# A blocked causal attention with a feed-forward layer behind it: a stored order of issue in place of a list scheduler

## The chip, the cores and the metric

The kernel runs on one core of a Trainium2 chip. The metric is the device time of one execution in microseconds, taken as the median of the runs; lower is better. The engines are TensorE (PE; its weight loads PEld), VectorE (DVE), ScalarE (ACT), GpSimd (POOL) and SyncE (SP). Loads and stores are issued from the queues of SyncE and ScalarE.

## What is computed

Attention over 8 batches of 8 heads, 576 tokens of 64 dimensions, masked by blocks of 64 tokens, and on its output, as 4608 tokens of 512 dimensions, a layer of width 2048 with a hard gate:

```python
def _attn_ref(q, k, v):            # (8, 8, 576, 64) each
    ...
    scores = scale * np.matmul(q, k.transpose(0, 1, 3, 2))
    mask = block_i >= block_j      # blocks of 64
    scores = np.where(mask, scores, -1000000000.0)
    ...
    attn = attn / (np.sum(attn, axis=-1, keepdims=True) + 1e-09)
    return np.matmul(attn, v)

def _moe_ref(x, w_in, w_out):      # 4608x512, 512x2048, 2048x512
    h = x @ w_in
    relu6 = np.clip(h + 3.0, 0.0, 6.0)
    g = h * relu6 / 6.0
    return g @ w_out
```

## The kernel before

Matmuls run in f16 on operands that are split into a high and a low part: a product is three matmuls (high with high, high with low, low with high), and each f16 matmul step is a row of pairs, one matmul for each half of the array's 128 columns. The attention of batch 0 and the first feed-forward piece (192 tokens) run in f32.

The work is cut so. Attention goes by pairs of heads (`n`, 32 of them) and by three groups of query blocks (`g`): `s_group` (L1465) makes the scores `s`, their row maxima (`st`, VectorE), the exponentials (`p`, ScalarE), scaled probabilities split into halves (`phl`), which a DMA transposes (`pT`); `pv_group` (L1579) multiplies with V (`vhl`) into `x`. `qk_load` and `qk_prep` (L1205, L1216) load and split q and k (`qks`, `qkT`). For the first batch the steps with 32 in their names do the same in f32 (`qf`, `qr`, `qt`, `sf`, `pf`, `pt`, `pr`, `rd`). The feed-forward layer goes by 13 pieces of up to 384 tokens and 16 slices of the width: `ffn1` (L1793) makes `h`, the gate (`r`) and its halves (`g`); `ffn2` (L1841) adds up the output `o` over the 16 slices. Pieces 11 and 12 form `h` from seven half-sized products `m` for each pair of slices (`h_pair`, L1733; `w_comb`, `x_comb` prepare the sums `wr`, `wq`, `ws`, `xr`, `xt`). The weights come in 64-bit form (`rawi`, `rawo`, and pieces of `x` as a buffer), are converted (`exi`, `exo` on ScalarE; `sgi`, `sgo` on GpSimd or VectorE), scaled by reductions over the whole core (`gm`, `gs`, `mb`, `mt`) and split into `win` and `wout`.

None of this is issued as it is written. `Recorder` (L422) takes the place of the engines and records every call as a step (`Op`), with the steps that it depends on (`touch`, L556) and the engines that could run it (`ways`): scalings may run on VectorE, ScalarE and often GpSimd, loads may be issued from SyncE or ScalarE. Consecutive matmuls of one `joint` are one step. There are 6396 steps.

`schedule` (L644) then orders them by a list scheduler. It has a cost for each call (`cost`, L588) and keeps a clock for each engine; whichever engine's clock is lowest picks, among the steps whose inputs are there and whose tiles find a buffer, the one with the smallest due time. Due times come from the kernel's plan and from `SHIFT` (L78), a number for each group of steps; `LEAN` (L243) adds to the choice of engine where a step has several ways. On TensorE a change between steps that write half of the array's columns and steps that write all of them costs `TURN`, and the half ones are gathered in bursts. `emit` (L847) issues the steps in the order of their start, so every instruction stands under one line, L851. The framework keeps that order on each engine, gives each tile a buffer in that order, and adds the waits.

Of the kernel before, what the change touches and what calls it, by code (L numbers as in the profile page):

```python
# [17 lines left out]
P = 128  # L18
# [6 lines left out]
U = 2.211  # L25
# [30 lines left out]
LANES = 8  # L56
# [21 lines left out]
SHIFT = {  # L78
# [318 lines left out]


class Op:

    __slots__ = ("ways", "key", "grp", "lean", "preds", "joint", "n", "start", "end", "tiles", "eng", "half")


class Engine:


    def __init__(self, rec, name):
# [1706 lines left out]
```

## Time and profile before

| | us |
|---|---|
| median of 3 runs | 989.18 (988.69 to 990.63) |
| span of the profiled execution | 987.2 |
| TensorE busy | 965.6 |
| VectorE busy | 887.3 |
| ScalarE busy | 628.9 |
| GpSimd busy | 75.1 |

The span goes from the first to the last instruction of the profiled execution; the time of a run has some 2 us around it. A row of a group names the line, the engine, the operation, the tile written and those read, their shapes and the count; then busy time, mean ns of one, and the idle time of the engine just before with what ended it. Names have their buffer numbers left out.

### The profile page before, as it was taken

To read this page: it belongs to the slowest core of one execution; us is meant where nothing else is said; L and a number is where in the kernel's file an instruction comes from. 1 tells how busy PE (TensorE), PEld (TensorE's weight loads), DVE (VectorE), ACT (ScalarE), POOL (GpSimd) and SP (SyncE) were. 2 spreads that over 40 slices of the span, in tenths; PEclk is the share of its full clock that TensorE was granted. 3 is DMA by queue.
4 is the path that set the end of the run, shared out by engine and by line. 5 is a ranking of instruction groups with operands and counts; after the bars stand their busy time and mean duration, and the time that the engine had idled before them with its cause. 6 is when DMAs were issued, how large, how long until landed. Compare 5 with 4: busy or idle time off the path is not lost.

```text
span 987.2 us, 31085 instructions
## 1 busy us (share of the span) xinstructions
PE 965.6 (98%) x12585; PEld 722.1 (73%) x12585; DVE 887.3 (90%) x2450; ACT 628.9 (64%) x1527; POOL 75.1 (8%) x242
## 2 busy tenths in 40 slices
PE   6899999999999999999999999999999999999998
PEld 5666567767778866776677776777677787878885
DVE  6999999999999999999999899988979879977864
ACT  4788877676676666777784766665667554534422
POOL 1133200000000000000000000000100102000000
PEclk9999999999999999999999999999999999999999
DMA  8965567979789799898999686776667451000000
GB/s 233 308 210 157 103 124 137 188 127 214 113 155 199 125 181 160 135 188 149 160 168 170 110 174 124 125 150 123 128 131 135 79 101 36 2 34 2 34 3 33
DMA packets 407183, 129.02 MB, mean 131 GB/s; under 512 B 393984, under 2 KB 396544, under 8 KB 407040
## 3 DMA queue, kind: packets, MB, share of 16 engines
q1 hardware_dynamic: 397520, 118.84, 63.0%
q10 hardware_dynamic: 9520, 8.21, 2.8%
q8 instruction: 98, 1.61, 0.7%
q14 instruction: 45, 0.37, 0.1%
HBM read 45.09 MB, written 9.44 MB: 55 GB/s over the span
## 4 chain that ended last, share of the span: by engine, by line
PE 70%; DVE 5%; ACT 1%; issue 1%; DMA 0%; SPq 0%; DVEq 0%; ACTq 0%
PE o L851 30%; PE h L851 24%; PE m L851 6%; PE s L851 5%; PE pv L851 5%; DVE st L851 1%; DVE phl L851 1%; ACT p L851 1%; DVE r L851 1%; DVE qks L851 1%; DMA qk<-in_k_dram 0%; DVE g L851 0%; DVE vhl L851 0%; DVE qkmx L851 0%; DVE x L851 0%
## 5 line engine op out<-in xcount | busy, mean ns | idle before, releaser
L851 PE MATMUL o<-wout,g 128*64 128x512 f16 (+3 forms) x3336 | 404.5, 378 | 0.0
L851 PE MATMUL h<-x,win 128*64 128x384 f16 (+2 forms) x3952 | 356.2, 319 | 1.7 <-DVE r L851 1.2
L851 PEld LDWEIGHTS <-win 128*64 128x64 f16 (+1 forms) x4440 | 270.0, 110 | 60.0 <-issue 4.2
L851 PEld LDWEIGHTS <-g 128*64 128x64 f16 x3360 | 218.8, 110 | 107.7
L851 ACT ACTIVATE p<-s,st,esc 128x384 f32<-128x384 f32 (+4 forms) x280 | 163.0, 587 | 62.7 <-DVE st L851 47.0
L851 ACT ACTIVATE r<-h,eg,sh 128x384 f32<-128x384 f32 (+1 forms) x192 | 112.0, 600 | 71.5 <-PE h L851 67.6
L851 DVE SCALAR_TENSOR_TENSOR phl<-p,st,phl 128x384 f16<-128x384 f32 (+4 forms) x252 | 138.6, 589 | 0.5 <-ACT phl L851 0.4
L851 DVE TENSOR_REDUCE st<-s 128x1 f32<-128x384 f32 (+4 forms) x280 | 117.8, 447 | 10.2 <-PE s L851 8.8
L851 DVE SCALAR_TENSOR_TENSOR g<-r,g 128x384 f16<-128x384 f32 (+1 forms) x192 | 102.9, 541 | 5.1 <-ACT g L851 3.9
L851 ACT ACTIVATE g<-r 128x384 f16<-128x384 f32 (+1 forms) x135 | 67.7, 506 | 53.7 <-DVE r L851 27.5
L851 DVE SCALAR_TENSOR_TENSOR r<-r,eg,h 128x384 f32<-128x384 f32 (+1 forms) x160 | 93.7, 588 | 7.4 <-ACT r L851 7.1
L851 PE MATMUL s<-qkT 128*64 128x512 f16 (+7 forms) x1120 | 96.6, 287 | 2.2 <-ACT p L851 2.1
L851 ACT ACTIVATE phl<-p,st 128x128 f16<-128x128 f32 (+4 forms) x147 | 77.2, 563 | 28.3 <-DVE st L851 15.6
L851 PEld LDWEIGHTS <-vhl 128*64 128x64 f16 x1680 | 72.0, 110 | 9.5 <-issue 2.3
L851 PEld LDWEIGHTS <-qkT 128*64 128x64 f16 x1120 | 58.8, 110 | 24.9 <-issue 4.9
L851 PE MATMUL pv<-pT,vhl 128*64 128x192 f16 (+2 forms) x1680 | 73.0, 233 | 1.3 <-ACT x L851 0.8
L851 POOL MEMSET p<- 128x64 f32 x140 | 22.8, 163 | 529.5 <-DVE phl L851 460.0
L851 ACT ACTIVATION_READ_ACCUMULATOR p<-s,st,esc 128x1 f32 x280 | 55.2, 197 | 0.0
L851 ACT ACTIVATE r<-hf,eg,sh 128x192 f32<-128x192 f32 (+1 forms) x48 | 26.4, 592 | 40.7 <-DVE hf L851 39.3
L851 DVE SCALAR_TENSOR_TENSOR qks<-qk,rs_q,qks 128x576 f16<-128x576 f32 x56 | 45.8, 834 | 0.1
L851 DVE TENSOR_SCALAR phl<-p,st 128x512 f16<-128x512 f32 (+4 forms) x105 | 41.8, 419 | 1.1 <-DVE st L851 0.2
L851 PE MATMUL m<-x,ws 128*64 128x192 f16 x768 | 39.0, 246 | 0.0
(191 smaller groups left out, 1036.6 us busy)
## 6 DMA issues: line engine op xcount, KB each, us to landing
out_dram<-osb SPq DMA_DIRECT2D x34, 256.0 KB, 2.4
qk<-in_q_dram SPq DMA_DIRECT2D x28, 288.0 KB, 3.8
qk<-in_k_dram SPq DMA_DIRECT2D x26, 288.0 KB, 4.5
vnat<-in_v_dram SPq DMA_DIRECT2D x58, 128.0 KB, 3.2
rawo<-in_moe_w_out_dram SPq DMA_DIRECT2D x9, 512.0 KB, 5.8
x<-in_moe_w_in_dram SPq DMA_DIRECT2D x5, 512.0 KB, 6.2
pT<-phl SPq DMA_TRANSPOSE x140, 3.7
rawi<-in_moe_w_in_dram SPq DMA_DIRECT2D x4, 512.0 KB, 6.0
```

Source lines behind the costliest of these rows:

```text
L851: getattr(eng, method)(*args, **kw)
```

## The change

`SHIFT`, `LEAN`, the costs and the list scheduler go. In their place stands `ORDER`, a packed table with one entry of two bytes for each of the 6396 steps: thirteen bits are the step's number as recorded, three bits its engine. `schedule` unpacks it and hands out the steps in that order, each on the engine that the table names. The recorder, the steps, their tiles and the plan that records them are the same. What differs on the chip is the place of a step in its engine's queue, and for some the engine:

| steps on | before | table |
|---|---|---|
| TensorE | 2108 | 2108 |
| VectorE | 2444 | 2240 |
| ScalarE (with loads) | 1219 | 1328 |
| GpSimd | 236 | 312 |
| SyncE (loads, stores, transposes) | 389 | 408 |

ScalarE's queue begins in the table with loads of `qf` (k, q), then `vnat` three times and `qf` (q) twice; after these seven comes its first step of work. SyncE's begins with one load of `vnat`, then `qf` (q, k, k, k) and the first weight piece `rawi`. In the trace of before ScalarE's queue begins with two loads of `vnat`, SyncE's with one.

```diff
--- before.py
+++ after.py
@@ -75,332 +75,144 @@
-SHIFT = {
-    0: -94, 2: 115, 3: -347, 4: -33, 5: -62, 6: -65, 7: 144, 8: 268, 11: -175, 12: 150, 13: 13, 14: -134,
...
-LEAN = {
-    20: (-1145, 0), 50: (1084, 0), 60: (195, 0), 70: (-42, 0), 80: (0, -166), 82: (0, -194), 83: (-32, 0),
...
+ORDER = (
+    "c-l=^1wb2Jv&B7-1g%jVLWm2rK!M;EAqifJyK99~+}-Q$Za_=j-Q7!D>h9Fu+zovHo9y1bGjq<Fxf`;A-#9~~@l@JETRRF_XR?;5"
...
+    "a5Q5i(+idHusKF`kf}Hz^-v?(aWpTZ8jVU}L8H;IEQsVn$4ZR#0}7#-KUQF@q|yHnGO$r-Z)h*1d;brADM2a"
+)
 class Op:
 
-    __slots__ = ("ways", "key", "grp", "lean", "preds", "joint", "n", "start", "end", "tiles", "eng", "half")
+    __slots__ = ("ways", "preds", "joint", "n", "eng")
...
 class Recorder:
     NAMES = ("tensor", "vector", "scalar", "gpsimd", "sync")
-    LAT = {"tensor": 855, "vector": 37, "scalar": 39, "gpsimd": 65, "sync": 65}
-    TURN = 95
-    BIAS = {"vector": 250.0, "gpsimd": 500.0}
-    EDGE = 0.0
-    BURST, PATIENCE = 3, 4000.0
-    POLL = {"tensor": 1.0, "vector": 20.0, "scalar": 20.0, "gpsimd": 150.0, "sync": 100.0}
-
     def __init__(self, nc):
         self.nc = nc
         self.ops = []
-        self.key = 0.0
-        self.cls = ""
-        self.grp = 0
-        self.part = {}
+        self.key, self.cls, self.grp = 0.0, "", 0
         self.joint = None
-        self.adv = ADV
-        self.share = 2
         for n in self.NAMES:
             setattr(self, n, Engine(self, n))
         self.hist = {}
-        self.meta = {}
-        self.users = {}
 
     @staticmethod
     def box(a):
...
@@ -517,33 +305,12 @@
         last = self.ops[-1] if self.ops else None
         if eng == "tensor" and self.joint is not None and last and last.joint == self.joint:
             op = last
-            calls, occ, _, _ = op.ways[eng]
-            more, took, _ = self.cost(eng, method, args, kw, outs, ins)
-            op.ways[eng] = (calls + [(method, args, kw)], occ + more, occ + took, False)
+            op.ways[eng].append((method, args, kw))
         else:
             op = Op()
-            op.joint, op.n, op.ways = None, len(self.ops), {}
...
-            op.key = self.key - self.adv.get((eng, self.cls), 0.0) 
-            op.grp = self.grp + (10000 if eng == "tensor" else 20000 if ways[0][1] == "dma_start" else 0)
-            op.key += 0.1 * SHIFT.get(op.grp, 0)
-            op.lean = self.BIAS
-            if len(ways) > 1:
-                part = self.part[op.grp] = self.part.get(op.grp, -1) + 1
-                dv, dp = LEAN.get(10 * op.grp + part, (0, 0))
-                if dv or dp:
-                    op.lean = dict(vector=self.BIAS["vector"] + dv, gpsimd=self.BIAS["gpsimd"] + dp)
-            op.preds, op.tiles, op.start = {}, [], None
-            op.half = eng == "tensor" and outs[0].ap[0][1] <= 64 and method == "matmul"
-            if eng == "tensor":
-                op.joint = self.joint
+            op.joint, op.n = self.joint if eng == "tensor" else None, len(self.ops)
+            op.ways = {e: call[0] if isinstance(call[0], list) else [tuple(call)] for e, *call in ways}
+            op.preds, op.eng = set(), None
             self.ops.append(op)
         for _, *call in ways[1:]:
             for _, a, k in call[0] if isinstance(call[0], list) else [call]:
@@ -556,298 +323,41 @@
     def touch(self, op, a, w):
         t = a.tensor
         p0, p1, b0, b1 = self.box(a)
-        if t.name not in self.meta:
-            self.meta[t.name] = str(t.tag), t.tag_meta.bufs
-            self.users[t.name] = []
-        u = self.users[t.name]
-        if not u or u[-1] != op.n:
-            u.append(op.n)
-            op.tiles.append(t.name)
         writes, reads = self.hist.setdefault(t.name, ([], []))
         for kind in (writes, reads) if w else (writes,):
             keep = []
             for e in kind:
                 o, q0, q1, c0, c1 = e
                 if o is not op and q0 < p1 and p0 < q1 and c0 < b1 and b0 < c1:
-                    op.preds[o.n] = op.preds.get(o.n, False) or kind is writes and not w
+                    op.preds.add(o.n)
                 if not (w and p0 <= q0 and q1 <= p1 and b0 <= c0 and c1 <= b1):
                     keep.append(e)
             if w:
                 kind[:] = keep
         (writes if w else reads).append((op, p0, p1, b0, b1))
 
...
-    def cost(self, eng, method, args, kw, outs, ins):
...
     def schedule(self):
...
-        while done < N:
-            e = min((x for x in self.NAMES if pend[x] or avail[x]), key=lambda x: now[x], default=None)
-            if e is None:
-                raise RuntimeError("no order")
...
-                            mine = t + ways[e][2] + ops[k].lean.get(e, 0.0)
-                            r = min(
-                                max(now[q], ready[k][q]) + ways[q][2] + ops[k].lean.get(q, 0.0)
-                                for q in ways if q != e
-                            )
-                            r = t if r >= mine else max(t + 50.0, t + mine - r)
...
-            if shared:
-                t = max(t, port["gpsimd" if e == "vector" else "vector"])
-                port[e] = t + took - 60.0
-            if e == "tensor" and o.half != half:
-                half = o.half
-                self.turns += 1
-                t += self.TURN
...
-        return sorted(ops, key=lambda o: (o.start, o.n))
+
+        import base64
+        import zlib
+
+        raw = zlib.decompress(base64.b85decode("".join(ORDER)))
+        half = len(raw) // 2
+        if half != len(self.ops):
+            raise RuntimeError(f"{half} steps in the table, {len(self.ops)} in the program")
+        done = set()
+        for lo, hi in zip(raw[:half], raw[half:]):
+            o = self.ops[lo + 256 * (hi % 32)]
+            o.eng = self.NAMES[hi // 32]
+            if o.n in done or not o.preds <= done:
+                raise RuntimeError(f"step {o.n} out of order")
+            done.add(o.n)
+            yield o
 
     def emit(self):
         for o in self.schedule():
             eng = getattr(self.nc, o.eng)
-            for method, args, kw in o.ways[o.eng][0]:
+            for method, args, kw in o.ways[o.eng]:
                 getattr(eng, method)(*args, **kw)
```

## Rows read from the trace of the kernel before

**Rows 1.** The page's first part: busy time, share of the span, instructions.
```profile
PE 965.6 (98%) x12585; PEld 722.1 (73%) x12585; DVE 887.3 (90%) x2450; ACT 628.9 (64%) x1527; POOL 75.1 (8%) x242
```

**Rows 2.** Busy time by stretch; the first line names the columns.
```profile
core 0: us, PE busy (x) PEld busy (x) DVE busy (x) ACT busy (x) POOL busy (x), PEclk, DMA share, GB/s
0.00:12.00 12.00, 4.70 (x64) 4.16 (x64) 5.73 (x16) 2.26 (x6) 2.16 (x19) 1.00 0.73 177
12.00:60.00 48.00, 44.07 (x525) 31.72 (x521) 41.69 (x117) 36.48 (x112) 8.17 (x17) 1.00 0.92 290
60.00:200.00 140.00, 136.34 (x1448) 92.79 (x1449) 135.86 (x408) 110.43 (x269) 23.86 (x47) 1.00 0.71 147
200.00:983.50 783.50, 780.49 (x10559) 593.39 (x10555) 703.55 (x1909) 479.28 (x1143) 40.88 (x159) 1.00 0.64 117
```

**Rows 3.** Chain that ended last: start us, us, what, count.
```profile
825.77 5.85 PE h L851 x72
831.62 7.77 PE o L851 x72
...
909.55 5.45 PE m L851 x132
```

**Rows 4.** TensorE's forms, 200 to 983.5 us: first and last of 23.
```profile
L851 PE MATMUL o<-wout,g 128*64 128x512 f16 x2976 | 353.9, 379 | 0.0
...
L851 PE MATMUL mb_v<-dg_v,one 1*64 1x1 bf16 x10 | 0.9, 185 | 0.0
```

**Rows 5.** The view by form, whole span: VectorE, ScalarE and GpSimd.
```profile
L851 DVE SCALAR_TENSOR_TENSOR g<-r,g 128x384 f16<-128x384 f32 x176 | 97.4, 558 | 4.8 <-ACT g L851 3.7
L851 DVE TENSOR_SCALAR g<-r 128x384 f16<-128x384 f32 x52 | 18.3, 353 | 8.1 <-PE o L851 7.8
...
L851 ACT ACTIVATE g<-r 128x384 f16<-128x384 f32 x124 | 63.9, 519 | 51.5 <-DVE r L851 25.3 <-PE o L851 25.3
...
L851 POOL TENSOR_TENSOR xr<-x 128x384 f32<-128x384 f16 x6 | 7.8, 1308 | 30.9 <-DVE phl L851 23.9 <-DVE x L851 5.9 <-DVE xt L851 1.1
L851 POOL TENSOR_SCALAR qks<-qks 128x576 f16<-128x576 f16 x8 | 6.1, 766 | 24.0 <-DVE qks L851 16.8 <-ACT qks L851 4.7 <-issue 2.5
L851 POOL TENSOR_SCALAR sgo<-rawo 128x512 int32<-128x512 uint32 x4 | 4.0, 1006 | 11.1 <-ACT pf L851 3.6 <-ACT qkf L851 3.4 <-DMA rawo<-in_moe_w_out_dram 3.1
```

**Rows 6.** Instructions in order of time, 0 to 12 us.
```profile
0.73 0.99 ACTq L851 DMA_DIRECT2D vnat<-in_v_dram  x2
...
1.53 0.58 SPq L851 DMA_DIRECT2D qf<-in_q_dram  x1
...
4.42 1.90 PE L851 MATMUL qt<-ident,qf 64*64 64x64 f32 x24 [4.42 <-DMA qf<-in_q_dram]
...
9.73 1.28 ACT L851 ACT_TABLE_LOAD   x1 [9.73 <-DMA qr<-in_k_dram]
...
11.03 0.33 ACT L851 ACTIVATE qkf<-qt 128x192 f32<-128x192 f32 x1
...
11.70 0.48 PE L851 MATMUL sf<-qkf 64*64 64x64 f32 x4 [1.80 <-ACT pf L851]
```

**Rows 7.** TensorE's waits, 12 to 200 us: total us, times, longest.
```profile
PE sf L851 <- ACT pf L851: 3.0, 3, 1.8
```

**Rows 8.** TensorE in order of time at 290 us.
```profile
289.95 0.69 PE L851 MATMUL h<-x,win 128*64 128x384 f16 x6
290.56 0.27 PE L851 MATMUL mt_v<-ident,vm 128*1 128x128 f32 x1
290.76 0.52 PE L851 MATMUL h<-x,win 128*64 128x384 f16 x4
```

**Rows 9.** TensorE's waits from 200 us on.
```profile
PE s L851 <- ACT p L851: 1.0, 2, 0.8
```

**Rows 10.** GpSimd and VectorE in order of time at 833 us.
```profile
832.57 2.77 POOL L851 TENSOR_TENSOR xr<-x 128x384 f32<-128x384 f16 x2 [5.87 <-DVE x L851]
...
834.49 1.26 DVE L851 SCALAR_TENSOR_TENSOR g<-r,g 128x384 f16<-128x384 f32 x1
```

More of the change, by code (lines that the diff above doesn't have):

```diff
@@ L416, in __getattr__ @@
         return call
-ADV = {("tensor", "a"): 60.0}
 class Recorder:
     NAMES = ("tensor", "vector", "scalar", "gpsimd", "sync")
-    LAT = {"tensor": 855, "vector": 37, "scalar": 39, "gpsimd": 65, "sync": 65}
-    TURN = 95
-    BIAS = {"vector": 250.0, "gpsimd": 500.0}
-    EDGE = 0.0
-    BURST, PATIENCE = 3, 4000.0
-    POLL = {"tensor": 1.0, "vector": 20.0, "scalar": 20.0, "gpsimd": 150.0, "sync": 100.0}
     def __init__(self, nc):
@@ L460, in box @@
         return p0, p0 + dims[0][1], f0 * sz, (f0 + n) * sz
-    @staticmethod
-    def count(a):
-        n = 1
-        for _, c in list(a.ap)[1:]:
-            n *= c
-        return n
     @staticmethod
@@ L519, in add @@
             op = last
-            calls, occ, _, _ = op.ways[eng]
-            more, took, _ = self.cost(eng, method, args, kw, outs, ins)
-            op.ways[eng] = (calls + [(method, args, kw)], occ + more, occ + took, False)
+            op.ways[eng].append((method, args, kw))
         else:
             op = Op()
-            op.joint, op.n, op.ways = None, len(self.ops), {}
-            for e, *call in ways:
-                calls = call[0] if isinstance(call[0], list) else [tuple(call)]
-                occ, took = 0.0, 0.0
-                for m, a, k in calls:
-                    more, last, port = self.cost(e, m, a, k, *self.operands(a, k))
-                    took = occ + last
-                    occ += more
-                op.ways[e] = (calls, occ, took, port)
-            op.key = self.key - self.adv.get((eng, self.cls), 0.0)
-            op.grp = self.grp + (10000 if eng == "tensor" else 20000 if ways[0][1] == "dma_start" else 0)
-            op.key += 0.1 * SHIFT.get(op.grp, 0)
-            op.lean = self.BIAS
-            if len(ways) > 1:
-                part = self.part[op.grp] = self.part.get(op.grp, -1) + 1
-                dv, dp = LEAN.get(10 * op.grp + part, (0, 0))
-                if dv or dp:
-                    op.lean = dict(vector=self.BIAS["vector"] + dv, gpsimd=self.BIAS["gpsimd"] + dp)
-            op.preds, op.tiles, op.start = {}, [], None
-            op.half = eng == "tensor" and outs[0].ap[0][1] <= 64 and method == "matmul"
-            if eng == "tensor":
-                op.joint = self.joint
+            op.joint, op.n = self.joint if eng == "tensor" else None, len(self.ops)
+            op.ways = {e: call[0] if isinstance(call[0], list) else [tuple(call)] for e, *call in ways}
+            op.preds, op.eng = set(), None
             self.ops.append(op)
@@ L577, in touch @@
         (writes if w else reads).append((op, p0, p1, b0, b1))
-    @staticmethod
-    def run(a):
-        n = 1
-        for st, c in reversed([x for x in list(a.ap) if x[1] > 1]):
-            if st != n:
-                break
-            n *= c
-        return n * mybir.dt.size(a.dtype)
-    def cost(self, eng, method, args, kw, outs, ins):
-        n = self.count(outs[0])
-        if method == "dma_start":
-            nb = mybir.dt.size(outs[0].dtype)
-            for _, c in list(outs[0].ap):
-                nb *= c
-            if kw.get("transpose"):
-                occ = max(1290, 172 * nb / 32768 - 150, 245 * nb / 32768 - 1215)
-                return occ, occ + 2100, False
-            if eng == "gpsimd":
-                return 1300, 2900 + nb / 170, False
-            run = min(self.run(outs[0]), self.run(args[1] if len(args) > 1 else ins[0]))
-            return 600, 2450 + nb / (205 if run <= 256 else 260 if run < 2000 else 320), False
-        if eng == "vector":
-            if method == "tensor_reduce":
-                n = self.count(ins[0])
-            else:
-                ptr = any(isinstance(a, bass.AP) and self.count(a) == 1 for a in args[2:] if n > 1)
-                ptr = ptr or n == 1 and method == "tensor_scalar_mul" and isinstance(args[2], bass.AP)
-            wide = [a for a in ins if self.count(a) > 1 and not self.psum(a)]
-            port = len(wide) > 1
-            if method in ("tensor_scalar", "tensor_copy") and n > 1:
-                if not any(self.psum(a) for a in outs + ins):
-                    if len(outs[0].ap) == 2 or outs[0].ap[1][1] % 2 == 0:
-                        n = n / (4 if mybir.dt.size(outs[0].dtype) + mybir.dt.size(ins[0].dtype) == 4 else 2)
-                        port = True
-            occ = 68 + 1.042 * n
-            if method != "tensor_reduce" and ptr:
-                occ += 57
-            return occ, occ + 80, port
-        if eng == "scalar":
-            occ = 94 + 0.8335 * n
-            if isinstance(kw.get("scale"), bass.AP):
-                occ += 95
-            if isinstance(kw.get("bias"), bass.AP):
-                occ += 58
-            if "accum_out" in kw:
-                occ += 93
-            return occ, occ + 105, False
-        if eng == "gpsimd":
-            if method == "memset":
-                return 20 + 1.0 * n, 50 + n, False
-            occ = 75 + (2.0 if method == "tensor_tensor" else 1.1) * n
-            return occ, occ + 30, True
-        f32 = mybir.dt.size(ins[0].dtype) == 4
-        occ = max(n / 2.37, 26) * (4 if f32 else 1) + 2
-        if f32 and method == "matmul":
-            occ = max(occ, 200)
-        if method == "transpose":
-            occ = max(occ / 2, 100)
-        if outs[0].ap[0][1] <= 64 and method == "matmul":
-            occ = occ / self.share
-        return occ, occ + 172, False
```

302 lines of the change are left out of this document (127 added, 175 removed), and 313 rows, old and new, of tables (LEAN, SHIFT).

## Prediction

> **What bounds the kernel now.** I read the page's busy shares first: TensorE is busy 98% of the span, VectorE 90%, ScalarE 64%, GpSimd 8% [rows 1]. A busy TensorE need not be a fast one, so the second view was busy time by stretch [rows 2]: its idle time is 7.3 us in the first 12 us, 3.9 us from there to 60, 3.7 us up to 200, and 3.0 us in the 783.5 us that follow. The granted clock is 1.00 in all four, the upper of its two levels, so the clock has no part in this. The third view, the chain that ended last, shows what a stretch without gaps costs [rows 3]: 72 second-layer matmuls of 512 columns in 7.77 us are 107.9 ns each, 72 first-layer ones of 384 columns in 5.85 us are 81.3 ns, 132 of 192 columns in 5.45 us are 41.3 ns. (Two matmuls, one on each half of the array, run side by side; these are times of one out of a row of such pairs.)
>
> These paces give a floor for the stretch from 200 us on. Its 23 forms with their counts are in the view by form, of which the first and the last stand here [rows 4]. Added up by columns: 3266 matmuls of 512 columns (2976 `o` of the first row, 90 more `o`, 200 `s`) at 107.9 ns are 352.4 us; 3200 of 384 columns (3102 `h`, 98 `s`) at 81.3 are 260.0; 2898 of 192 columns (`pv`, `m`, `h`, `s`) at 41.3 are 119.7; the 1136 others, at the same 0.21 ns a column, are 40.7. The sum is 772.8 of 783.5 us. So 80% of the kernel lies 10.7 us above the pace of its own bursts, and that is all that an order of issue can win there. I take 2.6 us of it to be the small scale reductions (`mb`, `mt`) that any order must place, which leaves 8 us.
>
> The Trainium skill (Perfetto Trace Analysis, Identifying the Most-Contended Engine) calls matmul busy share a poor measure of headroom and weight-load share a better one. The trace has 73% there [rows 1], which by that rule would leave up to 27% of the span, some 260 us (an estimate); the gapless bursts of [rows 3] show that there is no such room.
>
> **What the change does, in counts.** The table is read by its own rule (the upper three bits of a step's second byte are its engine) and each entry set beside the engine and place which the same step has in the trace of before. The steps stay the same, so each edit is a move.
>
> *Engines.* 183 steps go from VectorE to ScalarE and 55 to GpSimd; 34 come back from ScalarE to VectorE; 34 go from ScalarE to GpSimd and 13 from there to ScalarE. The steps that leave VectorE are scalings such as `g`, 353 ns [rows 5]; at about 0.4 us, 238 of them are some 95 us, and some 14 us come back: 887 goes to about 805 us. ScalarE pays 519 ns for the same `g` [rows 5]: 196 more and 68 fewer steps are about 65 us, 629 to 695. GpSimd gets 89 and loses 13: 22 integer conversions at 1.0 us, 25 `qks` copies at 0.77 [rows 5], 8 sums of 1024 elements at some 3.5 us (an estimate from 1.3 us for 384 elements [rows 5]), the rest short: 75 goes to about 160 us. All three stay below TensorE, so these sums cost nothing by themselves; what counts is which wait of TensorE ends sooner or later.
>
> *Start.* Before, V is loaded first, the first loads of q and k go out behind it at 1.5 us and later, and TensorE starts at 4.42 us [rows 6]. In the table ScalarE's queue begins with loads of q and k, SyncE's has them behind one load of V: the first matmul gains little, I say 0.2 us. But before, ScalarE issues 13 loads ahead of its table load at 9.73 us; its first result comes at 11.03 and TensorE waits 1.8 us for a softmax block, until 11.70 [rows 6]. The table leaves ScalarE seven loads before its first step. I drop that wait: 2.0 us for the start, bounds 0 (another wait, for a transfer, takes its place) and 3. SyncE gets 30 loads from ScalarE and gives back 11; what stands behind a load there waits with it for its buffer. The first weight piece goes out sixth on SyncE's queue, where it stood behind eleven loads on ScalarE's, so I expect no loss from that.
>
> *12 to 200 us.* TensorE idles 7.6 us [rows 2]. The waits are many and short, the longest group 3.0 us for softmax results [rows 7]. The DMA engines are 92% busy between 12 and 60 us, VectorE 97% between 60 and 200 [rows 2]; the first can't be reordered away, the second is eased by some 20 us. I take half: 3.8 us, bounds minus 4 and 7.6.
>
> *Switches of width.* Most f16 matmuls write one half of the array's 128 columns each, the f32 transposes and a few others all of them. Along TensorE's order the change of kind falls from 116 to 74 times, nearly all of the 42 ahead of 200 us. One stands at 290 us [rows 8]: six `h` from 289.95 us at 81.3 ns would end at 290.44, the odd matmul starts at 290.56, the next `h` 0.20 us behind that. So some 0.1 us each, 4.2 us for 42. Where a switch falls into a wait it is free; I take 3 us, bounds 0 and 5. Changes between the f16 kinds (`o`, `h`, `pv`, `s`) grow in number by some 400; I cost them at nothing, since the chain passes from `h` to `o` at 831.62 us without a gap [rows 3].
>
> *From 200 us on.* For each TensorE step I took the matmul work queued between the last TensorE step that its inputs come from and itself, less the durations of the other engines' steps on the way (no queueing counted). Under 0.5 us of such room is left for 53 steps in the old order and for 25 in the table. That speaks for fewer waits, and the VectorE work that ScalarE takes over, mostly here, for shorter queues ahead of what TensorE needs. The waits that show are short again, the longest group 1.0 us [rows 9]; the rest of the 10.7 us is in gaps too small for that view. I take half of 8: 4 us, bounds minus 2 and 8.
>
> *GpSimd beside VectorE.* This speaks against. From 832.57 to 835.34 us GpSimd works on two sums, and VectorE's `g` residual beside them takes 1.26 us [rows 10], where its mean is 0.56 [rows 5]. So a GpSimd step can add 0.7 us to VectorE, and 89 more are between 0 and 62 us on it, against some 80 net that it sheds. Only early, where VectorE is 97% busy, do I charge the path for it: 2 us, bounds 0 and 12. The Trainium skill (SBUF — State Buffer, SBUF: two separate sides) says that the port pair the two engines share is locked for a whole instruction, and that a VectorE instruction with two SBUF inputs waits for it. The lengthened row agrees in kind; that each of the 89 blocks VectorE for its whole length is shown by no row.
>
> **Sum.** 2.0 + 3.8 + 3 + 4 - 2 = 10.8 us. The profiled execution spans 987.2 us and the median of the runs is 989.2 us, so 2.0 lie around the span and stay: 976.4 us of span, 978.4 us of time. The tail behind the last matmul keeps its steps.
>
> **Rivals.**
> 1. Everything recoverable is recovered: 3 + 7.6 + 5 + 8 = 23.6 us, 965.6 us. For it: the table's room in front of TensorE. Against: part of the early idle time is transfers.
> 2. Bytes and latencies hold the early part whatever the order: nothing between 12 and 200 us, the switches saved lay in waits anyway; 2 us at the start and 3 late remain, 984.2 us. For it: DMA engines at 92%, 290 GB/s [rows 2].
> 3. Waits are moved, not removed; each chain that is served sooner makes another late: 989 us. Against it: the room counted above.
> 4. Slower, by GpSimd's hold on VectorE ahead of 200 us: some 55 of the new GpSimd steps lie there; if half meet a VectorE step that must wait, by the 0.7 us of [rows 10], that is 19 us, about what VectorE sheds there. But VectorE works in order, and behind the blocked step stands what TensorE waits for. If two thirds reach TensorE, 13 us come on; with only the start's 2 and the late 4 won the time is 996 us. It decides from about 9 of the blocks reaching TensorE (6 us). For it: VectorE at 97%. Against it: what moves there is weight preparation with time in hand.
>
> **How the numbers follow.** Forecast (970 to 983): 0.50. Rival 1: 0.15. Rival 2: 0.20. Rival 3: 0.07. Rival 4: 0.08. Faster by over 0.2% (about what a measurement of this kernel can tell from no change) are the first three, 0.85; within 0.2%: 0.07; slower: 0.08. The range goes from 967, most of the way to rival 1, to 987.5, past rival 2; it leaves out rivals 3 and 4 and a little below.
>
> **What will show it.** Right: TensorE idle about 5 us in the first 12, a first ScalarE result ahead of 8 us; idle near 4 us between 12 and 200; from 200 us to the last matmul some 7 us above the floor of its counts; VectorE near 805, ScalarE near 695, GpSimd near 160 us. Wrong: TensorE waiting early for VectorE beside long GpSimd steps (rival 4); a new long wait for a transfer (then the order of loads is what I misjudged); idle time between 12 and 200 us unchanged (rival 2).

## The result, and the profile after

The changed kernel takes 1003.71 us (median of 4 runs, 1002.1 to 1007.19). The kernel before, timed beside it, takes 989.90 (4 runs). The ratio is 1.0149, with a 95% interval of 1.0127 to 1.0171. Where I forecast 10.8 us less, 14 us more came out. The profiled execution spans 1001.9 us against 987.2.

The page's first line answers [rows 1]; busy time by stretch, under it, answers [rows 2].

```profile
PE 967.5 (97%) x12585; PEld 702.9 (70%) x12585; DVE 839.4 (84%) x2246; ACT 691.1 (69%) x1655; POOL 140.9 (14%) x318
```

```profile
core 0: us, PE busy (x) PEld busy (x) DVE busy (x) ACT busy (x) POOL busy (x), PEclk, DMA share, GB/s
0.00:12.00 12.00, 4.44 (x60) 3.74 (x60) 2.29 (x7) 3.27 (x10) 2.50 (x17) 1.00 0.68 167
12.00:60.00 48.00, 44.15 (x490) 32.36 (x490) 36.42 (x102) 32.27 (x96) 21.70 (x37) 0.93 0.84 254
60.00:200.00 140.00, 133.78 (x1462) 92.49 (x1458) 132.44 (x375) 112.59 (x275) 46.77 (x77) 1.00 0.70 151
200.00:983.50 783.50, 770.47 (x10433) 564.56 (x10429) 661.94 (x1749) 537.29 (x1268) 69.89 (x187) 1.00 0.66 119
```

The matmuls are the same 12585 and their busy time hardly moved; what grew is the time between them. In the long last stretch TensorE idles 13.0 us where it idled 3.0. VectorE, ScalarE and GpSimd shifted as the table says, and VectorE is *less* busy than before.

To find the place, I worked out a gap for each TensorE step: the distance from its start to the next step's start, less the shortest distance that such a step ever shows. The steps are the same in every kernel here, and their shortest distances add up to 946.0 us, so beside the start of the first step (4.42 us before, 4.01 after) the gaps are what differs. By stretch, in us (time lost to a lower clock is in them too):

| kernel | 0-12 | 12-60 | 60-200 | 200-340 | 340-450 | 450-740 | 740-820 | behind | all |
|---|---|---|---|---|---|---|---|---|---|
| before | 3.9 | 9.9 | 10.8 | 2.8 | 1.2 | 2.8 | 0.8 | 0.7 | 32.9 |
| after | 4.1 | 11.8 | 11.2 | 2.8 | 5.5 | 1.5 | 2.0 | 9.2 | 48.0 |

Of the 15.1 us, 8.5 arise behind 820 us, 4.3 between 340 and 450, 2.5 ahead of 200. From 450 to 740 the new order is 1.3 us better. TensorE's waits from 200 us on, which answer [rows 9], are headed by one of `pv` (total us, times, longest):

```profile
PE pv L361 <- DVE x L361: 7.9, 4, 2.9
PE m L361 <- DVE hu L361: 1.3, 2, 0.7
PE h L361 <- DVE r L361: 1.2, 3, 0.6
```

`pv`, the matmul that multiplies the softmax with V, waits for `x`, the step that *reads* a `pv` tile. Here is that place in order of time on TensorE, VectorE and ScalarE (start us, us, instruction, in brackets the idle time before it and who ended it):

```profile
828.55 0.29 PE L361 MATMUL pv<-pT,vhl 128*64 128x64 f16 x6
831.74 0.69 PE L361 MATMUL pv<-pT,vhl 128*64 128x192 f16 x6 [2.91 <-DVE x L361]
...
846.85 0.61 PE L361 MATMUL pv<-pT,vhl 128*64 128x192 f16 x12 [2.43 <-DVE x L361]
```

```profile
830.81 0.60 DVE L361 SCALAR_TENSOR_TENSOR r<-r,eg,h 128x384 f32<-128x384 f32 x1
831.34 0.35 DVE L361 TENSOR_SCALAR x<-pv 128x192 f16<-128x192 f32 x1
...
838.41 0.88 DVE L361 SCALAR_TENSOR_TENSOR phl<-p,st,phl 128x640 f16<-128x640 f32 x1 [4.94 <-ACT phl L361]
...
846.44 0.35 DVE L361 SCALAR_TENSOR_TENSOR x<-pv,x 128x192 f16<-128x192 f32 x1
```

```profile
836.99 0.67 ACT L361 ACTIVATE r<-h,eg,sh 128x384 f32<-128x384 f32 x1 [4.91 <-PE h L361]
```

One tile `pv31` holds two ranges of 192 columns, each the sum of its own matmuls. At 828.84 us the first range is done. The matmul into the *second* range stands next on TensorE and needs nothing of the first, yet starts 0.05 us after VectorE's read of the first has ended. The compiled program has a wait on VectorE there. The recorder's own list of dependencies, by which the table was made valid and by which I measured "room", compares columns and has no such edge. While TensorE stands, no `h` is made; ScalarE idles 4.91 us for it, and VectorE, which has the next step queued behind ScalarE's `phl`, idles 4.94. The second read, whose input has been ready since 831.7, then comes at 846.44, and TensorE stops again. There are five such waits in the changed kernel, 9.2 us together by the gaps: 0.95 us at 365.0, 0.59 at 386.3, 1.95 at 748.3, and the two above. (That all gaps behind 820 us are also 9.2 us is chance: only the two above, 5.7 us, lie there.) The one at 365.0 us is not the read's alone: in e1 and e9 below, which take the read out of its way, the same matmul still stops 0.82 and 0.61 us, for a transfer (`pT`). The kernel before has three, of 0.62 us each by the gaps; here is one in its trace:

```profile
824.78 0.33 ACT L851 ACTIVATE x<-pv 128x192 f16<-128x192 f32 x1 [0.47 <-PE pv L851]
```

```profile
825.16 0.60 PE L851 MATMUL pv<-pT,vhl 128*64 128x192 f16 x12 [0.42 <-ACT x L851]
```

Read alone, 0.42 us of this kind looks like any other short wait; but `x` is no input of `pv`. The stops themselves are thus 7.3 us (9.2 less 1.9) of the 15.1; the rest is in other waits.

Second, from 820 to 860 us VectorE had next to no idle time before. Rows of before, then of after (columns as above):

```profile
820.00:860.00 40.00, 39.58 (x554) 31.97 (x551) 39.24 (x79) 20.00 (x39) 5.03 (x4) 1.00 0.12 23
```

```profile
820.00:860.00 40.00, 34.66 (x410) 26.35 (x408) 30.52 (x62) 19.02 (x36) 12.94 (x9) 0.96 0.16 30
```

Before, VectorE was busy 39.24 of 40 us here, while [rows 2] averaged it to 90% of the whole last stretch; in the changed kernel it idles 9.5 us of them. But a full VectorE is no mark of this place. Two other pieces of before:

```profile
220.00:260.00 40.00, 39.15 (x522) 31.04 (x520) 40.00 (x111) 28.15 (x68) 1.68 (x9) 1.00 1.03 178
500.00:540.00 40.00, 40.00 (x513) 31.14 (x510) 39.63 (x107) 26.08 (x64) 2.19 (x11) 1.00 1.03 177
```

There it was fuller, and in their stretches (200 to 340 and 450 to 740 us) the new order loses nothing.

Third, the clock. From 12 to 60 us the granted clock is 0.93, where [rows 2] have 1.00: it is at the lower of its two levels (1.2 GHz) from 29.3 to 36.2 us. Ahead of that TensorE had been busy 7.36 of 9.3 us, with one wait of 1.21 us:

```profile
20.00:29.30 9.30, 7.36 (x104) 5.09 (x100) 7.76 (x23) 5.53 (x19) 3.96 (x10) 1.00 0.88 260
29.30:36.20 6.90, 6.90 (x42) 3.80 (x39) 4.43 (x13) 3.44 (x12) 2.41 (x3) 0.51 0.94 318
```

It fell again at 831.5 us, in the wait of 2.91 us above, for 3.4 us. In e5's profile below TensorE was busy only 6.76 us of the same 9.3, and the clock did not fall there.

### The profile page after: what moved, and what is told of

Same layout as the page of the kernel before. It is cut to its first block, busy times and chain, and to the rows that moved or that the text cites. A ratio compares the mean times of both kernels' runs of the same rounds, so it can differ in the third digit from the quotient of the medians.

```text
span 1001.9 us, 31115 instructions
## 1 busy us (share of the span) xinstructions
PE 967.5 (97%) x12585; PEld 702.9 (70%) x12585; DVE 839.4 (84%) x2246; ACT 691.1 (69%) x1655; POOL 140.9 (14%) x318
## 5 line engine op out<-in xcount | busy, mean ns | idle before, releaser
L361 PE MATMUL o<-wout,g 128*64 128x512 f16 (+3 forms) x3336 | 429.7, 379 | 1.7 <-DVE g L361 0.9
L361 PE MATMUL h<-x,win 128*64 128x384 f16 (+2 forms) x3952 | 381.1, 319 | 1.2 <-DVE r L361 1.2
L361 PEld LDWEIGHTS <-win 128*64 128x64 f16 (+1 forms) x4440 | 258.3, 110 | 79.3 <-issue 3.3
L361 ACT ACTIVATE p<-s,st,esc 128x384 f32<-128x384 f32 (+5 forms) x280 | 162.9, 586 | 41.4 <-DVE st L361 32.6
L361 ACT ACTIVATE phl<-p,st 128x256 f16<-128x256 f32 (+4 forms) x217 | 118.8, 582 | 40.1 <-DVE st L361 21.2
L361 DVE TENSOR_REDUCE st<-s 128x1 f32<-128x384 f32 (+6 forms) x280 | 120.6, 448 | 14.9 <-PE s L361 14.7
L361 ACT ACTIVATE g<-r 128x384 f16<-128x384 f32 (+1 forms) x167 | 83.2, 505 | 43.8 <-DVE r L361 28.1
L361 PE MATMUL s<-qkT 128*64 128x64 f16 (+7 forms) x1120 | 101.0, 287 | 1.9 <-DMA qkT<-qks 1.3
L361 PE MATMUL pv<-pT,vhl 128*64 128x192 f16 (+2 forms) x1680 | 84.8, 234 | 10.0 <-DVE x L361 7.9
L361 POOL TENSOR_SCALAR qks<-qks 128x576 f16<-128x576 f16 x30 | 23.6, 789 | 139.3 <-DVE qks L361 72.1
```

What stands on the lines that cost most here:

```text
L361: getattr(eng, method)(*args, **kw)
```

## The experiments

All are tables for the same steps, in another order or with other engines; the diffs show decoded entries (place in the order, engine, step). The kernel before, written as such a table, gives the same steps in the same order on every engine, so the table as a form should cost nothing; no run has it alone. Gaps are by the stretches above; "gaps behind" are those behind 820 us.

### Whose loss is it: reads, GpSimd, order, engines

**e1_reads_last.** The reads of eight `pv` tiles (twelve reads) go behind the tile's last matmul, and six steps that use them behind that; of `pv31`:

```diff
-5683 vector x3 <- pv31 (first columns)
 5684 tensor pv31 (second columns)
-5729 vector x3 residual <- pv31 (first columns)
 5744 tensor pv31 (second columns, last)
+     vector x3 <- pv31
+     vector x3 residual <- pv31
```

> The changed kernel's table with 13 steps moved back: the reads of a pv tile (x, and x's residual) come behind the last matmul of that tile, and what uses them behind that; engines as in the table. Theory A (a matmul into a pv tile waits for every read of the tile issued ahead of it, though the columns differ): the five waits of TensorE for x, 9.2 us, go, and with the longest of them the drop of the clock at 831 us: 992 to 996 us. Theory B (GpSimd's steps hold up VectorE and so TensorE): those waits only change their name, 1001 to 1004 us.

Measured: 1002.97 us, ratio 1.0127 [1.0107, 1.0147]. The waits for `x` are gone and so is the late fall of the clock; gaps behind fall from 9.2 to 5.0, but those of 340 to 450 us grow from 5.5 to 6.9, and 450 to 740 from 1.5 to 2.7. TensorE's waits from 200 us on:

```profile
PE h L356 <- DVE r L356: 4.6, 7, 1.3
PE m L356 <- DVE hu L356: 2.0, 2, 1.4
PE pv L356 <- DMA pT<-phl: 1.2, 2, 0.8
PE h L356 <- ACT x L356: 0.8, 1, 0.8
```

The wait can be taken away and the time stays: other waits take its place, one of them (the last row, at 413 us) for a read that is now late itself. Theory A has these waits and the clock right, theory B the time.

**e2_gpsimd_back.** 89 steps go back from GpSimd to the engines of before, in the changed order:

```diff
-gpsimd wr1 ... wr7, conversions of weights, qks copies (89 steps)
+vector or scalar, as in the kernel before
```

> The changed kernel's table, every step in its place, but the 89 steps that it newly puts on GpSimd go back to the engine that they had before (55 to VectorE, 34 to ScalarE). Theory A: the order of pv matmuls and reads stays, so most of the loss stays: 999 to 1006 us, with the waits of TensorE for x still there. Theory B: 991 to 996 us.

Measured: 1016.22 us, ratio 1.0261 [1.0239, 1.0283]; `pv` still waits 7.6 us for `x`. The time is outside both ranges. Within this order, taking GpSimd's steps back regains nothing: the kernel loses 12 us more.

**e3_before_reads_last.** The edit of e1 in the order and with the engines of before.

> The order and engines of the kernel before, written as a table, with only the reads of each pv tile held behind its last matmul. Theory A: the three gaps of 0.62 us inside pv rows (at 336, 772 and 825 us of the trace of before) go: 1 to 2 us faster than before, 988 us. Theory B: no change, 990 us.

Measured: 992.15 us, ratio 1.0028 [1.0019, 1.0036]. The three stops of 0.62 us vanish (gaps 0.8 to 0.1 and 0.7 to 0.3 from 740 us on), but 340 to 450 us grows from 1.2 to 4.5, and the time is outside both ranges. The edit holds back sixteen reads of ten tiles, of which three had a stop; the tiles between 340 and 450 us had none, and `h` and `s` now wait for their reads there (1.1 us in three waits). So this run prices the reads held back, not the stops.

**e4_engines_only** and **e11_order_only.** Order of before with the new engines, and the new order with the engines of before:

```diff
-order: table      engine of each step: table
+order: before     engine of each step: table     (e4)
+order: table      engine of each step: before    (e11)
```

> The order of the kernel before with the engines of the changed table: one part of the change alone. Theory A: the order does the harm, so 987 to 993 us. Theory B: the engines do it, 997 to 1004 us.

> The changed kernel's order of issue with the engines of the kernel before for every step. Theory 1 (order and engines were found together, and either alone misfits): slower than the changed kernel, 1005 to 1025. Rival (the choice of engines is the fault): 988 to 998.

Measured: 1019.17 us, ratio 1.0298 [1.0279, 1.0317], and 1063.74 us, 1.0743 [1.0705, 1.078]. Both are above every range given. Either half alone is far worse than both together, with gaps of 65.8 and 111.9 us against 48.0. In both many engines are waited for, in small pieces; TensorE's longest groups from 200 us on, e4 first:

```profile
PE s L362 <- ACT p L362: 6.6, 11, 1.5
PE h L362 <- DVE r L362: 3.1, 6, 1.4
```

```profile
PE pv L356 <- DVE x L356: 5.2, 3, 2.5
PE pv L356 <- DMA pT<-phl: 5.1, 3, 2.5
PE h L356 <- DVE r L356: 4.8, 10, 1.2
```

So order and engines were fitted to each other. What one of them is worth can't be priced alone, as I did.

### Which stretch

**e5_reads_early.** The same reads go forward instead of back, directly behind what they need; ten of the twelve change their place by it:

```diff
+5681 vector x3 <- pv31 (first columns)
+5682 vector x3 residual <- pv31 (first columns)
-5683 vector x3 <- pv31 (first columns)
 5684 tensor pv31 (second columns)
-5729 vector x3 residual <- pv31 (first columns)
```

> The table of the changed kernel with its engines; only the twelve ScalarE and VectorE reads of a pv tile that stand ahead of a later matmul into that tile are moved forward, to directly behind the last matmul they depend on (the largest moves are 49 and 28 places, the others 1 to 18). Theory 1 (the loss from 340 us on is the wait of that later matmul for reads that come late in their engine's queue; 9.2 us in five waits): the reads end earlier wherever the queue lets them, the waits of pv for x fall from 7.9 us to 3 to 5, time 997 to 1001. Rival (VectorE is so far behind there that the read's place matters little, it is the work queued ahead of it that sets the end of the read): the waits stay at 6 us or more, time 1001 to 1006.

Measured: 1003.40 us, ratio 1.0144 [1.0129, 1.0159]: the rival's time, though `pv`'s waits for `x` fall to 3.3 us, as theory 1 said. The second stop is gone, the first stays, since VectorE is 2 us behind with what stands ahead of the read, and other waits come in; gaps behind are 7.9.

```profile
831.07 0.69 PE L356 MATMUL pv<-pT,vhl 128*64 128x192 f16 x6 [2.76 <-DVE x L356]
```

This run has something else to tell. Its first 200 us are the changed kernel's, and in its profile the clock stayed up there:

```profile
12.00:60.00 48.00, 43.03 (x505) 32.39 (x506) 37.72 (x107) 33.95 (x99) 21.36 (x37) 1.00 0.87 261
```

The gaps from 0 to 200 us are then 4.2 + 9.6 + 10.5 = 24.3 us, against 24.6 before: that, and no more, is what the new order gains there.

**e6_before_to_200, e7_before_from_740, e8_five_parts.** Order and engines by stretch:

```diff
-after's table throughout
+before's to 200 us, after's from there                                    (e6)
+after's to 740 us, before's from there                                    (e7)
+before's to 200, after's to 340, before's to 450, after's to 740, before's (e8)
```

> Order and engines of the kernel before for all that it had begun by 200 us, those of the changed kernel for the rest. Theory 1 (losses belong to the stretch in which they arise and add up): the changed kernel stood 1 to 2.3 us behind at 200 us, so the time falls by that from 1003.7 to 1001 to 1003, and the granted clock keeps full speed around 30 us. Rival (the early part is where the later backlog of VectorE and ScalarE comes from): the late losses shrink too, time 990 to 997.

> Order and engines of the changed kernel for all that the kernel before had begun by 740 us, those of the kernel before for the rest. Theory 1 (losses belong to their stretch): the changed kernel stood about 5 us behind at 740 us, and from there the order of before adds nothing, so 993 to 996. Rival (the backlog that the changed kernel carries into 740 us makes the losses behind it): the time stays above 998.

> Order and engines by stretch, each stretch being the steps that the kernel before had begun in it: before's for 0 to 200 us, the changed kernel's for 200 to 340, before's for 340 to 450, the changed kernel's for 450 to 740, before's from 740 on. Theory 1 (losses and gains belong to their stretch): gaps of 2.67 us instead of 2.67 in 200 to 340 and of 1.34 instead of 2.67 in 450 to 740, so 1.3 us less than before: 987 to 989. Rival (order and engines fit only as a whole; each seam costs as the mixed order and engines did): 992 to 1000.

Measured: e6 1002.66 us, ratio 1.0140 [1.0127, 1.0153]; e7 995.56, 1.0068 [1.0056, 1.0080]; e8 992.47, 1.0038 [1.0026, 1.0051]. e7 bears out theory 1: with before's order from 740 us on the gaps behind are 0.7, though the kernel comes there 5 us late. The loss of the last part is made in it. e6 has theory 1's time and does not bring back the late part (gaps behind 7.2). Its profile also shows one point of my expectation wrong: the clock fell in it, for 13.7 us, under before's own first 200 us of steps. So the fall is not the new order's alone; the mean clock of the five timed executions of e7 is 0.994 to 0.997, of eleven of before beside them nine have 1.000. But none of e6's four executions has 1.000 either (0.993 to 0.998), so that it comes more often with the new start is not shown. Why it comes, I leave open. e8's time is the rival's, 3.5 us above theory 1's range: its gaps are 2.9 for 340 to 450 us (1.35 of them in one gap at 339.6 us, where two parts join) and 2.4 for 450 to 740, where theory 1 put 1.2 and 1.5, and 2.1 for 740 to 820 (before: 0.8). Part of what a stretch costs comes from what it is joined to, as the rival has it.

### The wait without its side effects

**e9_matmuls_first.** Neither read is moved. The matmuls behind it go ahead of it:

```diff
+5683 tensor pv31 (second columns)
+     tensor pv31 (second columns, two more)
 5683 vector x3 <- pv31 (first columns)
-5684 tensor pv31 (second columns)
 5729 vector x3 residual <- pv31 (first columns)
-5743 tensor pv31 (second columns)
-5744 tensor pv31 (second columns, last)
```

and so for five more tiles, 17 steps in all.

> The changed kernel with 17 matmul steps moved forward in the table: the matmuls into the second column range of six pv tiles (13, 14, 15, 28, 30, 31) stand directly ahead of the first read of the tile that they stood behind, by 1 to 62 places; no read, engine or other step is moved. Theory 1 (TensorE stopping for a read of other columns of the tile starts the loss: while it stops, ScalarE and VectorE run dry behind it, and VectorE has no time to make that up between 820 and 880 us): pv's waits for x fall from 7.9 us to under 1 us, VectorE's idle 4.9 us at 833 us goes, the loss behind 740 us falls from 10 us to 1 to 3 us, time 994 to 998. Rival (as with the reads moved, another wait takes the place): time 1000 to 1004.

Measured: 999.28 us, ratio 1.0096 [1.0076, 1.0117]: 4.4 us less than the changed kernel, from 17 moved steps of 6396. No `pv` waits for `x`, the clock stays up at 831 us, ScalarE's and VectorE's idle times of 4.91 and 4.94 us there are down to 0.71 and 0.74, and gaps behind fall from 9.2 to 4.3. That is half of what theory 1 expected and outside what either theory gave: its mechanism is borne out by the waits, its size is not. Half of it goes the rival's way, to other waits: `h` for `r` grows from 1.2 to 3.3 us, `pv` waits 2.4 for `pT`. What is left behind 820 us is in these lines of TensorE:

```profile
851.08 0.68 PE L356 MATMUL h<-x,win 128*64 128x384 f16 x6 [1.25 <-DVE r L356]
...
860.06 1.18 PE L356 MATMUL m<-x,ws 128*64 128x192 f16 x24 [1.37 <-DVE hu L356]
```

**e10_before_matmuls_first.** The same edit in the order of before: seven matmul steps of `pv12`, `pv29` and `pv31`, by 1 to 14 places.

> The kernel before as a table of its own order and engines, with seven matmul steps of three pv tiles (12, 29, 31) moved 1 to 13 places forward, ahead of the read that they stood behind. Theory 1 (the three stops of 0.62 us are nothing but that wait): 1.9 us less than before, 986.8 to 988. Rival (the read that follows now starts later and its reader waits): within 0.5 us of before.

Measured: 987.91 us (11 runs), ratio 0.9985 [0.9973, 0.9998]. It is faster than both kernels, if by little: the gaps from 740 us on are 0.2 instead of 1.5, and no stop is left in front of `pv`:

```profile
823.01 1.20 PE L360 MATMUL pv<-pT,vhl 128*64 128x192 f16 x30
824.01 2.79 PE L360 MATMUL h<-x,win 128*64 128x384 f16 x32
```

### GpSimd beside VectorE

VectorE's and GpSimd's instructions in order of time, from e9's profile:

```profile
837.36 0.61 DVE L356 SCALAR_TENSOR_TENSOR r<-r,eg,h 128x384 f32<-128x384 f32 x1 [0.88 <-ACT r L356]
...
845.67 2.24 DVE L356 SCALAR_TENSOR_TENSOR g<-r,g 128x384 f16<-128x384 f32 x1
...
854.41 2.89 DVE L356 SCALAR_TENSOR_TENSOR ws<-wq,ws 128x1024 f16<-128x1024 f32 x1 [0.19 <-ACT ws L356]
```

```profile
836.63 2.13 POOL L356 TENSOR_TENSOR wr<-win 128x1024 f32<-128x1024 f16 x1 [3.33 <-DVE wq L356]
...
845.38 2.12 POOL L356 TENSOR_TENSOR wr<-win 128x1024 f32<-128x1024 f16 x1 [1.89 <-DVE wq L356]
...
853.43 2.78 POOL L356 TENSOR_TENSOR wr<-win 128x1024 f32<-128x1024 f16 x1 [4.75 <-DVE wq L356]
```

What [rows 10] hinted at is larger here: the `g` residual takes 2.24 us instead of the 0.56 of [rows 5] while GpSimd makes the sum `wr`. It ends at 847.91 us, 0.41 behind the end of the sum (847.50), and `ws` at 857.30, 1.09 behind its sum (856.21); the row of [rows 10] has 0.41 too (835.75 after 835.34). So such a step seems to stand until the sum is done and then to run. Steps that read PSUM beside SBUF do not: `r` keeps its 0.61 us at 837.36, inside the sum from 836.63 to 838.76. Of the steps that VectorE has in both kernels, the 105 that start between 820 and 880 us before add up to 55.8 us before, 61.7 in the changed kernel, 62.5 in e9. Two runs move only the seven sums `wr1` to `wr7`:

```diff
-gpsimd wr1 ... wr7        (order of e9)
+vector wr1 ... wr7        (e12)
-vector wr1 ... wr7        (order of e10)
+gpsimd wr1 ... wr7        (e13)
```

> The kernel with the 17 matmul steps moved forward, and of its engines seven steps set back from GpSimd to VectorE: the sums wr of the weight halves (128x1024), made from 790 to 900 us. With them on GpSimd the 105 VectorE steps that both kernels give to VectorE between 820 and 880 us took 61.7 us in the changed kernel and 62.5 in the one with matmuls moved, against 55.8 before; single ones took 2.24 and 2.89 us instead of 0.55 and 1.21. Theory 1 (what is left of the loss behind 820 us, 4.3 us of gaps, is VectorE slowed beside GpSimd): those steps return to about 56 us, the gaps behind 820 us fall to 1 to 2 us, time 996 to 998. Rival (VectorE has no room for seven more steps of 1.2 us): the gaps stay or grow, time 1000 to 1004.

> The kernel before with seven matmul steps moved forward, and the same seven sums wr set from VectorE to GpSimd, everything else as it was. Theory 1 (GpSimd beside VectorE gives nothing back: VectorE's other steps grow by about as much as it is spared, and each wr takes 2.1 us instead of 1.2): 0 to 4 us slower than without the move, 988 to 992. Rival (VectorE, 97% busy between 820 and 880 us, is freed of 8 to 9 us of work): TensorE has no gaps to give back there, so within 0.5 us, 987.4 to 988.4, with VectorE idle for 5 us or more in the stretch.

Measured: e12 1000.40 us, ratio 1.0106 [1.0089, 1.0124]; e13 990.99, 1.0016 [1.0007, 1.0026]. e13 is theory 1: 3.1 us slower than e10, from nothing but the seven steps. Each takes 2.1 to 2.6 us instead of 1.2, and VectorE's 105 other steps grow from 55.6 to 60.4 us. Whether the longer sums or the longer steps make the 3.1 us, no run separates. Rows of e10 and e13, 820 to 860 us:

```profile
820.00:860.00 40.00, 40.00 (x566) 32.56 (x564) 39.78 (x83) 19.60 (x36) 5.03 (x4) 1.00 0.16 23
```

```profile
820.00:860.00 40.00, 37.95 (x525) 30.39 (x522) 37.12 (x72) 20.60 (x41) 13.04 (x9) 1.00 0.17 23
```

TensorE loses 2 us of 40 while VectorE gets emptier: of the 8.9 us that it is spared, 4.8 return as longer steps. And e10's row has a VectorE busy 39.78 of 40 us beside a TensorE without a gap: full alone, it costs nothing. The Trainium skill (SBUF — State Buffer, SBUF: two separate sides) has the engine that comes first hold the shared ports for a whole instruction. The ends of the single steps above agree. The sum over all steps is smaller than the time that GpSimd works: seven sums, 15.9 us, lengthened the 105 others by 4.8.

e12 is the rival's time. The 105 steps return to 55.1 us, as theory 1 said, but the gaps behind stay (4.4). So the price of GpSimd is real in before's order, and taking it back mends nothing in the changed order. What holds the last 4.3 us stays open. In both kernels VectorE idles for ScalarE's `r` between 815 and 900 us, 6.1 us in e9 and 5.4 in e12, in five waits each; that points at the places of these two engines' steps, which no run moved by themselves. No run takes the 4.3 us of 340 to 450 us apart either (two of the five stops, 1.5 us, lie there); after's own waits there are six groups of at most 0.9 us. e7 keeps that loss (5.7 us of gaps), e8, with before's order there, has 2.9.

## Why the prediction was wrong

**What bounds the kernel** was right as far as it went: the matmul work is fixed (946.0 us of shortest distances), and there was little to win. The same sum should have warned me on the other side. An order with 8 us to win and hundreds of engine moves has far more to lose. I read the last 783.5 us as one stretch [rows 2]; cut in pieces of 40 us, it shows VectorE at 98% from 820 to 860, where the change lost most, though not there alone. (In the floor, the 1136 other matmuls at 0.21 ns a column are 39.5 us and not 40.7, so the room was 11.9 us; that changes nothing.)

**Start, 2.0 us: failed.** The signs came: ScalarE's table load is at 5.28 us instead of 9.73, its first result at 6.57 instead of 11.03 [rows 6]. The gain did not, because the other end of my bound took its place, a transfer:

```profile
4.01 1.55 PE L361 MATMUL qt<-ident,qf 64*64 64x64 f32 x24 [4.01 <-DMA qf<-in_q_dram]
6.96 0.92 PE L361 MATMUL sf<-qkf 64*64 64x128 f32 x12 [1.40 <-ACT qkf L361]
9.84 1.97 PE L361 MATMUL qt<-ident,qf 64*64 64x64 f32 x24 [1.97 <-DMA qf<-in_q_dram]
```

The second block of transposes starts at 9.84 us. Before, its main part had started at 7.31. Gaps 4.1 us against 3.9; the first matmul came 0.41 us sooner, so the start won 0.2 us.

**12 to 200 us, 3.8 us, and switches of width, 3 us, less 2 for GpSimd: failed.** With the clock up (e5) the gaps of this stretch are 20.1 us against 20.7: 0.6 us of the 4.8. Waits moved. [Rows 7]'s 3.0 us for softmax results are gone, and in their place is, in the changed kernel,

```profile
PE pr L361 <- POOL rd L361: 3.1, 3, 1.2
PE pv L361 <- DMA pT<-phl: 1.4, 1, 1.4
PE s L361 <- DMA qkT<-qks: 1.3, 1, 1.3
```

The first waits for GpSimd. The 42 switches saved can't be seen in the sum, as rival 2 said. I had called the granted clock no part of this; in the changed kernel's profile, with the fall, the gaps of this stretch are 23.0 us, 2.9 more than in e5's.

**From 200 us on, 4 us: this step failed most.** The stretch lost 12.7 us (gaps 21.0 against 8.3). The room I measured came from the recorder's edges and "no queueing counted". Both halves of that were wrong. The wait of a matmul for reads of other columns is not among the edges: five stops, 9.2 us, against 1.9 before; e9, which removes nearly all of them, wins 4.4 us back and e10 1.4. The other part of the 12.7 us stays open; e4 and e11 show only that it hangs on order and engines together. And queueing is what makes a late read: the step is ready at 828.84 us and runs at 831.34, because VectorE is 2.5 us behind. "53 steps to 25" was true of a model that neither the chip nor the program follows. The engines I costed at nothing, "all three stay below TensorE", with the cover named as time in hand; from 820 to 860 us VectorE had 0.8 us in hand.

**GpSimd beside VectorE, 2 us, and rival 4.** The mechanism is right, the place was wrong. I charged it ahead of 200 us, where e5 shows no loss; it costs 3.1 us, by the gaps all behind 820 us, in e13. The sums took 2.1 us, not my 3.5. Rival 4 had the sign and half the size (996 us), for a reason that does not hold in the changed kernel: GpSimd's steps taken back regain nothing (e2, e12).

**Rival 3** (waits moved, not removed) is what happened nearly everywhere, in e1, e3, e5, e12 too. I gave it 0.07 and put it at no change. What it lacked is that a wait can grow as it moves; on what that depends, no run shows.

**Engine sums.** ScalarE came to 691.1 us (forecast 695), GpSimd 140.9 (160), VectorE 839.4 (805). I took 0.4 us for a step that leaves VectorE, but its successor starts before it has ended (831.34 + 0.35 against 831.61 above), so a step frees less than its duration; and the steps that stayed grew: those of both kernels from 200 us on add up to 767.4 us instead of 759.3.

## What to carry to other kernels

An order of issue is only as good as the list of edges it was searched with. Before trusting it, compare that list with the waits that the compiled program has, above all for tiles of which one part is read while another is written; where a matmul stands behind such a read, move the matmul ahead, not the read back. And look for slack in pieces of some 40 us: an engine at 90% over 780 us can be at 98% where the change lands. A full piece is a question, not an answer: others as full lost nothing. And order and engines that were found together can't be priced, or kept, one without the other.

## What the runs showed of the machine that I had not expected

- A matmul into columns 192 to 383 of a PSUM tile does not start until reads of columns 0 to 191 have ended, 0.05 us behind the read (831.74 after 831.69). It is a wait in the program; whether the chip would need it, no run shows. It costs 0.62 us when the read is prompt and 2.9 when the reader is behind.
- VectorE's instructions grow unevenly beside GpSimd's sums: single ones from 0.56 to 2.24 us and from 1.31 to 2.89 (means of before, single steps of e9), each ending 0.41 or 1.09 us behind the sum, while `r`, which reads PSUM, keeps 0.61 us. On average it is only 0.7 us of VectorE time for each sum of 2.1 to 2.6 us (4.8 us for seven, in e13).
- The granted clock can fall by half within a run of small f32 matmuls in some executions of one and the same program and not in others (29.3 to 36.2 us in the changed kernel's profile, not in the same first 200 us in e5's). e8's timed executions with a mean clock of 1.000 took 991.26 to 991.98 us, those with 0.996 or 0.997 took 992.96 to 994.56: 1 to 3 us for it.
